# A Fourier mix followed by eight routed experts: one weaving step moved, one small copy moved to another engine, and shorter planning instructions

## The chip, the cores and the metric

The kernel runs on one core of one Trainium2 chip. The metric is device microseconds of one execution, lower is better; the time before is the median of 3 runs, 1263.31 us (1263.24 to 1265.31). The engines are named as the profile names them: PE is TensorE's matmul, PEld its weight load, DVE is VectorE, ACT is ScalarE, POOL is GpSimd, SP is SyncE, which here only issues DMAs, in order.

## The reference

`x` has 8 batches of 2496 rows of 256 numbers. Each batch goes through a Fourier transform along its rows and one along its columns, of which the real part is kept. The 19968 rows that come out are routed:

```python
logits = x @ w_gate                       # 8 experts
expert_idx = np.argmax(logits, axis=1)
gate_w = softmax(logits)[chosen expert]
h = np.maximum(x_of_expert @ w1[e], 0.0)  # 256 -> 1024
y = h @ w2[e]                             # 1024 -> 256
out = gate_w[:, None] * y
```

Everything is computed in float32.

## The kernel before, in words

**Stages of a batch.** `first(b)` (line 325) does the transform along the rows: three pieces `q`, each a load `xq` from `x` (line 289), adds and subtracts on DVE that fold it (lines 294 to 309), two halves of matmuls into a tile `s` (lines 311 to 321), an ACT copy of each half to `t` (line 321) and a store of `t` to a scratch tensor `Td` in DRAM (line 342), after which the next batch's piece is loaded (line 344). `first` is a generator with 12 steps. After them `ahead_of(b)` (line 929) issues two loads from `Td` in another layout, tile `t4` (`regroup`, line 351), the profile's `t<-Td`.

`second(b)` (line 361) is a generator with 19 steps. Its first matmul is `pr` on `t4` (line 371). Then come matmuls into `p2` (copied by ACT to `zz`, line 379) and ten blocks of 128 positions with matmuls into `p3`. From each `p3` the kernel takes: `zs`, copied by ACT (line 405); the 2 x 8 logits `lg`, copied by DVE (line 408); and two result rows per position, made by DVE with two instructions that read `p3` and `zs` into `rows` (line 410). ACT then fills the other half of these rows by mirroring (`mirror`, line 383; it is called for the block before, after `zs` of this one). After five blocks `route` (line 416) takes the maximum of the logits on DVE, makes a one-hot tile `oh`, ranks rows with small matmuls into `rk`, and computes the place of each row. `send` (line 462) then has POOL scatter 128 rows at a time into `Xs`, a DRAM tensor sorted by expert (line 236). 

`s`, `p2`, `p3`, `pr` and `rk` share one pool of three PSUM buffers, each a bank, so a matmul into one of them waits until the reads of the tile that had it before are done.

**Plans.** `plan` (line 478) works on one partition of DVE: it finds out how many blocks of a given size each expert can fill, and writes a table of up to MOST = 21 entries with the place and the expert of each block. SP reads the table to fetch rows (`xb`, line 535) and weights (`w_sb`, lines 545 and 547) of a block. Plans ask for 2 and 4 blocks in batch 0, 4 in batch 1, 3 in batch 2, 5 in each of batches 3 to 6, and 5, 7 and 21 in batch 7.

**Experts.** `experts` (line 729) goes through 66 blocks of 512, 256 or 128 rows. For each: transpose on DVE (line 583), a sign on ACT (line 586), matmuls into `ph` (or, for some 512-row blocks, seven products instead of eight, lines 614 to 658), relu on ACT or DVE (`hT`, lines 837 and 839), matmuls into `py`, a scaled ACT copy to `y` (line 891), a POOL scatter to the output. Row and weight fetches run up to three blocks ahead.

**What sets the order.** All instructions are written out in an order fixed in advance, and each engine runs its own in that order. `mixed(b)` (line 935) weaves `second(b)` with `first(b + 1)`:

```python
one, two = ahead_of(b + 1), second(b)
for _ in range(3):
    next(one, None); yield
for k, _ in enumerate(two):
    if k % 2:
        next(one, None)
    yield
yield from woven(close(b), one)      # close: the plans of batch b
yield from through(b)
```

The main loop (lines 996 to 1026) draws steps of `mixed(b)` in between the matmul groups of the experts of batch b - 1, about one step for each four to eight matmuls. Batch 0 is woven with batch 1 by a loop of its own (lines 990 to 993).

Of the kernel before, what the change touches and what calls it, by code (L numbers as in the profile page):

```python
# [15 lines left out]
ALU = mybir.AluOpType  # L16
ACTF = mybir.ActivationFunctionType
AX_X = mybir.AxisListType.X
# [17 lines left out]
E, F = 8, 1024  # L36
# [6 lines left out]
NY = H + 1  # L43
# [3 lines left out]
def free(ap, offset, *dims):  # L47
    return bass.AP(ap.tensor, ap.offset + offset, [list(ap.ap[0])] + [list(d) for d in dims])


def bc(ap, axis, n):
    shape = list(ap.shape)
    shape.insert(axis, n)
    return ap[tuple([slice(None)] * axis + [None])].to_broadcast(shape)
# [75 lines left out]
def rounds():  # L130

    want = [((256, 2), (128, 4)), ((256, 4),)] + [((512, B),)] * (B - 2)
    plan, used = [], 0

    def full(done, size):
        return max(0, -(-(done - used - E * (size - 1)) // size))

    for b in range(B):  # L140
        done = (b + 1) * S
        now = []
        for size, most in want[b]:
            k = min(full(done, size), most)
            if k:
                now.append((size, k, False))
            used += size * k
        if b == B - 1:
            k = full(done, BLK)
            used += BLK * k  # L150
            now.append((BLK, k, False))
            now.append((REST, (NT - used + E * (REST - 1)) // REST, True))
        plan.append(now)
    return plan
# [33 lines left out]
MOST = max(k for now in rounds() for _, k, _ in now)  # L188
# [27 lines left out]
def kernel(ctx: ExitStack, tc, x, w_gate, w1, w2, out):  # L216
    nc = tc.nc
    vec, act, pool = nc.vector, nc.scalar, nc.gpsimd

    def mm(o, lhsT, rhs, start=True, stop=True, **kw):  # L220
        nc.tensor.matmul(o, lhsT=lhsT, rhs=rhs, start=start, stop=stop, **kw)  # L221
# [47 lines left out]
    con, k = {}, 0  # L269
# [91 lines left out]
    def second(b):  # L361

        t4 = None

        def turn_last(h):

            nonlocal t4
            t4 = ahead.pop((b, "t4", h))
            n = min(HALF, NG - h * HALF)
            pr = pm_.tile([GP, HALF], F32, tag="m", name="pr")  # L370
            mm(pr[:, 0:n], con["rot"][:], t4[0:GP, 0:n, H])
            act.copy(t4[0:GP, 0:n, H], pr[:, 0:n])

        def group(g):
            i, n = g % HALF, LAST if g == NG - 1 else GP
            p2 = pm_.tile([128, 2, n], F32, tag="m", name="p2")
            for c in range(2):
                mm(p2[:, c], t4[0:GP, i, c * H:(c + 1) * H], con["m2"][:, c, 0:n])
            act.copy(zz[:, :, g * GP:g * GP + n], p2[:])
            if g == HALF - 1:  # L380
                turn_last(1)

        def mirror(rows, k):
            act.copy(free(rows[:], (k + 1) * W + D - 1, [-W, 2], [-1, H - 1]),
                     free(rows[:], k * W + 1, [W, 2], [1, H - 1]))

        turn_last(0)
        yield
        group(0)
        yield  # L390
        group(1)
        yield
        for h in range(2):
            rows = sp.tile([128, NSL, W], F32, tag="rows", name="rows")
            lg = sp.tile([128, NSL, E], F32, tag="lg", name="lg")
            for i in range(HW):
                w, k = HW * h + i, 2 * i
                if w + 2 < NG:
                    group(w + 2)
                p3 = pm_.tile([128, 2 * NY + 2 * E + 1], F32, tag="m", name="p3")  # L400
                z = zz[:, :, 128 * w:128 * (w + 1)]
                mm(p3[:, 0:NY + 2 * E], z[:, 0], con["rd"][:, 0, 0:NY + 2 * E], True, False, skip_group_check=True)
                mm(p3[:, NY:], z[:, 1], con["rd"][:, 1], False, True, skip_group_check=True)
                zs = sp.tile([128, NY + 1], F32, tag="zs", name="zs")
                act.copy(zs[:], p3[:, NY + 2 * E:])  # L405
                if i:
                    mirror(rows, k - 2)
                vec.tensor_copy(lg[:, k:k + 2], p3[:, NY:NY + 2 * E].rearrange("p (m e) -> p m e", m=2))  # L408
                for m, op in enumerate((ALU.add, ALU.subtract)):
                    vec.scalar_tensor_tensor(rows[:, k + m, 0:NY], p3[:, 0:NY], zs[:, 0:1], zs[:, 1:],  # L410
                                             op0=ALU.add, op1=op)
                yield
            mirror(rows, k)
            yield from route(b, h, rows, lg)
# [60 lines left out]
    bk = {n: bt[:, lo:hi] for n, (lo, hi) in where.items()}  # L475
    gone = bk["cap"]

    def plan(b, size, k, last):

        nonlocal gone  # L480

        def one(name, *dims, dt=F32):
            return cp.tile([1, *dims], dt, tag="p_" + name, name="p_" + name, bufs=2 if name == "gone" else 1)

        nb, ni = one("nb", E), one("ni", E, dt=I32)
        ce, ex, rb, n = one("ce", E), one("ex", E), one("rb", E), one("n", E)
        lo = one("lo", E, E)
        vec.tensor_tensor(nb[:], base[0:1], gone[:], op=ALU.subtract)
        vec.tensor_scalar(ni[:], nb[:], size - 1.0 if last else 0.0, None, op0=ALU.add)
        vec.tensor_scalar(ni[:], ni[:], size.bit_length() - 1, None, op0=ALU.logical_shift_right)  # L490
        vec.tensor_copy(nb[:], ni[:])
        vec.tensor_tensor(lo[:], bk["low"].rearrange("p (a b) -> p a b", a=E), bc(nb[:], 1, E), op=ALU.mult)
        vec.reduce_sum(ce[:], lo[:], axis=AX_X)
        vec.tensor_tensor(ex[:], ce[:], nb[:], op=ALU.subtract)
        yield
        vec.scalar_tensor_tensor(rb[:], ex[:], -float(size), gone[:], op0=ALU.mult, op1=ALU.add)
        ge, ei = one("ge", MOST, E), one("ei", MOST)
        val, eq, rw = one("val", MOST, E + 1), one("eq", MOST, E + 1), one("rw", MOST)
        vec.tensor_tensor(ge[:], bc(bk["i"], 2, E), bc(ce[:], 1, MOST), op=ALU.is_ge)
        vec.reduce_sum(ei[:], ge[:], axis=AX_X)  # L500
        yield
        vec.tensor_tensor(eq[:], bc(ei[:], 2, E + 1), bc(bk["e9"], 1, MOST), op=ALU.is_equal)
        vec.memset(val[:, :, E:E + 1], float(E * CAP))
        vec.scalar_tensor_tensor(val[:, :, 0:E], bc(bk["i"], 2, E), float(size), bc(rb[:], 1, MOST),
                                 op0=ALU.mult, op1=ALU.add)
        yield
        vec.tensor_tensor(val[:], val[:], eq[:], op=ALU.mult)
        vec.reduce_sum(rw[:], val[:], axis=AX_X)
        tab = cp.tile([1, 2, MOST], I32, tag="p_tab", name="p_tab", bufs=4)
        vec.tensor_copy(tab[:, 0], rw[:])  # L510
        vec.tensor_scalar(tab[:, 1], ei[:], E - 1.0, None, op0=ALU.min)
        if last:
            cnt = cp.tile([1, 1], I32, name="cnt")
            vec.tensor_copy(cnt[:], ce[:, E - 1:E])
            tabs["cnt"] = cnt
        if not last:

            vec.tensor_scalar(n[:], ex[:], -1.0, float(k), op0=ALU.mult, op1=ALU.add)
            vec.scalar_tensor_tensor(n[:], n[:], 0.0, nb[:], op0=ALU.max, op1=ALU.min)
            nxt = one("gone", E)  # L520
            vec.scalar_tensor_tensor(nxt[:], n[:], float(size), gone[:], op0=ALU.mult, op1=ALU.add)
            gone = nxt
        yield
        tabs[b, size, last] = tab
# [384 lines left out]
    def woven(*parts):  # L909
        parts = list(parts)  # L910
        while parts:
            for p in list(parts):
                if next(p, p) is p:
                    parts.remove(p)
                else:
                    yield

    def close(b):

        for size, k, last in rounds()[b]:  # L920
            yield from plan(b, size, k, last)

    def through(b):

        while waiting and waiting[0][0] == b:
            yield
        whole.add(b)

    def ahead_of(b):

        yield from first(b)
        regroup(b, 0)
        regroup(b, 1)

    def mixed(b):

        one, two = (ahead_of(b + 1) if b + 1 < B else iter(())), second(b)
        for _ in range(3):
            next(one, None)
            yield  # L940
        for k, _ in enumerate(two):
            if k % 2:
                next(one, None)
            yield
        yield from woven(close(b), one)
        yield from through(b)
# [133 lines left out]
```

## Time and profile before

| what | value |
|---|---|
| median of 3 runs | 1263.31 us (1263.24 to 1265.31) |
| the profiled execution's own time | 1264.13 us |
| its span, first to last instruction | 1262.3 us |
| PE busy | 1214.1 us (96%), 7289 matmul instructions |
| DVE busy | 777.0 us (62%) |
| ACT busy | 424.8 us (34%) |
| POOL busy | 446.1 us (35%) |
| mean granted TensorE clock | 0.971 |
| DMA | 249.79 MB, mean 198 GB/s |
| DVE copies of logits, line 408 | x80, 13.8 us, mean 173 ns |

A row of the costliest groups names the line, the engine, the operation, what it writes and reads and how often, then busy time and the mean of one, then the idle time of the engine just before these instructions and what ended most of it. A line of the waits view reads "who waited <- for what: us in total, times, longest". A timeline line gives start, duration, engine, line, operation, and in brackets the idle time before it with its releaser. A busy PE is not PE at its peak, and its ends are modelled.

### The profile page before, as it was taken

How to read it: one execution, taken by the hardware profiler on the slowest of the kernel's cores; microseconds unless marked ns; L12 is line 12 of the kernel's file. 1: busy time of each engine (PE TensorE's matmuls, PEld its weight loads, DVE VectorE, ACT ScalarE, POOL GpSimd, SP SyncE). 2: the span in 40 equal slices, each digit the busy share in tenths (PEclk: the TensorE clock that was granted, in tenths of full speed). 3: DMA queues.
4: the chain of work that ended last, by engine and by line, in shares of the span. 5: the costliest groups of instructions: out<-in, count | busy, mean ns of one | idle time of the engine just before them, and what ended most of it. 6: DMA issues, size and time to landing. Idle time of an engine off the chain costs nothing.

```text
span 1262.3 us, 22196 instructions
## 1 busy us (share of the span) xinstructions
PE 1214.1 (96%) x7289; PEld 1080.3 (86%) x7289; DVE 777.0 (62%) x1884; ACT 424.8 (34%) x1087; POOL 446.1 (35%) x527
## 2 busy tenths in 40 slices
PE   5769999999999999999999999999999999999997
PEld 3658988777788899888988898889999999999996
DVE  4546334443466788576866578686888784444663
ACT  1423332332243433433344333432333232222222
POOL 0245436154116512472225603472364241111112
PEclk6759999999999999999999999999999999999998
DMA  8869898765348454573336435453346338788887
GB/s 236 272 195 327 304 307 306 204 224 169 126 147 258 138 142 160 154 263 115 101 123 207 141 94 160 140 179 101 105 138 190 109 105 282 284 289 275 285 284 278
DMA packets 163216, 249.79 MB, mean 198 GB/s; under 512 B 118601, under 2 KB 130227, under 8 KB 143516
## 3 DMA queue, kind: packets, MB, share of 16 engines
q1 hardware_dynamic: 146327, 203.28, 51.0%
q0 software_dynamic: 15888, 42.14, 9.3%
q10 hardware_dynamic: 885, 2.94, 0.7%
q8 instruction: 59, 0.97, 0.3%
q14 instruction: 57, 0.47, 0.1%
HBM read 194.91 MB, written 54.83 MB: 198 GB/s over the span
## 4 chain that ended last, share of the span: by engine, by line
PE 62%; issue 17%; DVE 10%; DMA 5%; POOL 4%; ACT 2%; POOLq 0%; SPq 0%; DVEq 0%; ACTq 0%
PE py L221 18%; PE a L221 9%; PE c L221 7%; PE ph L221 6%; PE p L221 6%; PE b L221 5%; PE d L221 4%; PE s L221 3%; PE e L221 3%; POOL out_dram L236 3%; DMA t<-Td 1%; DMA xq<-in_x_dram 1%; POOL Xs L236 1%; DVE xT L583 1%; DMA Td<-t 1%
## 5 line engine op out<-in xcount | busy, mean ns | idle before, releaser
L236 POOL DMA_INDIRECT out_dram<-y,ro x163 | 160.9, 987 | 629.5 <-ACT y L679 299.6
L221 PE MATMUL py<-w_sb,hT 128*128 128x256 f32 x1504 | 340.3, 380 | 0.0
L221 PEld LDWEIGHTS py<-w_sb,hT 128*128 128x128 f32 x1504 | 281.2, 190 | 36.9 <-issue 1.0
L236 POOL DMA_INDIRECT Xs<-rows,pi x160 | 164.2, 1026 | 111.7 <-DVE rows L410 53.0
L221 PE MATMUL ph<-xT,w_sb 128*128 128x128 f32 (+2 forms) x992 | 173.1, 330 | 10.0 <-DVE ro L792 8.8
L221 PEld LDWEIGHTS ph<-xT,w_sb 128*128 128x128 f32 x992 | 137.6, 194 | 34.4 <-issue 16.5
L221 PE MATMUL a<-xT,w_sb 128*128 128x256 f32 (+1 forms) x512 | 117.9, 357 | 0.0
L837 DVE TENSOR_SCALAR hT<-ph 128x512 f32<-128x512 f32 x43 | 29.7, 691 | 127.9 <-PE ph L221 68.2
L586 ACT ACTIVATE xT<-xT 128x256 f32<-128x256 f32 (+1 forms) x94 | 36.5, 388 | 181.7 <-DVE xT L583 137.3
L221 PEld LDWEIGHTS a<-xT,w_sb 128*128 128x128 f32 x512 | 88.5, 190 | 10.0 <-DVE xT L583 0.3
L891 ACT ACTIVATE y<-py,xb 128x256 f32<-128x256 f32 x94 | 44.5, 473 | 153.8 <-PE py L221 152.1
L635 DVE TENSOR_TENSOR hT<-hT,b 128x512 f32<-128x512 f32 x57 | 39.2, 687 | 79.0 <-PE b L221 53.4
L408 DVE COPY lg<-p 128x16 f32<-128x16 f32 x80 | 13.8, 173 | 111.4 <-ACT zs L405 111.3
L645 ACT ACTIVATE hT<-a 128x512 f32<-128x512 f32 x57 | 34.0, 597 | 134.1 <-PE a L221 131.1
L221 PE MATMUL s<-xq,w 104*112 104x256 f32 (+2 forms) x208 | 62.4, 425 | 11.8 <-DVE xq L297 9.5
L469 POOL CAST pi<-due 128x1 int32<-128x1 f32 x140 | 42.2, 302 | 68.4 <-ACT due L468 68.4
L221 PE MATMUL a<-w_sb,hT 128*128 128x128 f32 x528 | 66.0, 276 | 0.0
L221 PEld LDWEIGHTS p<-table,t 120*128 120x128 f32 x352 | 54.7, 206 | 10.6 <-issue 3.1
L221 PEld LDWEIGHTS a<-w_sb,hT 128*128 128x128 f32 x528 | 63.1, 192 | 0.7
L221 PE MATMUL c<-xT,ws 128*128 128x256 f32 (+1 forms) x256 | 60.2, 362 | 1.2 <-DVE hT L641 0.4
L221 PE MATMUL p<-table,zz 128*128 128x145 f32 (+1 forms) x320 | 57.6, 306 | 3.6 <-DVE rows L410 2.4
L583 DVE STREAM_TRANSPOSE xT<-xb 128x512 f32<-128x512 f32 (+1 forms) x91 | 56.3, 631 | 7.0 <-DMA xb<-Xs 7.0
(149 smaller groups left out, 2103.2 us busy)
## 6 DMA issues: line engine op xcount, KB each, us to landing
w_sb<-in_moe_w_dram SPq DMA_DIRECT2D x132, 1024.0 KB, 6.9
xq<-in_x_dram SPq DMA_DIRECT2D x24, 896.0 KB, 8.9
xb<-Xs SPq DMA_DIRECT2D x112, 128.0 KB, 3.3
Td<-t SPq DMA_DIRECT2D x18, 448.0 KB, 3.3
t<-Td SPq DMA_DIRECT2D x8, 768.0 KB, 7.0
t<-Td SPq DMA_DIRECT2D x8, 640.0 KB, 9.3
xb<-Xs SPq DMA_DIRECT2D x52, 64.0 KB, 4.7
xb<-Xs SPq DMA_DIRECT2D x88, 32.0 KB, 4.8
```

The costliest lines, as they stand in the source:

```text
L221: nc.tensor.matmul(o, lhsT=lhsT, rhs=rhs, start=start, stop=stop, **kw)
L236: return unordered(pool.indirect_dma_start(out=dst, out_offset=bass.IndirectOffsetOnAxis(ap=idx, axis=0), in_=rows, in_offset=None, bounds ...
L408: vec.tensor_copy(lg[:, k:k + 2], p3[:, NY:NY + 2 * E].rearrange("p (m e) -> p m e", m=2))
L469: pool.tensor_copy(idx, due[:])
L583: vec.transpose(free(xT[:], 256 * h, [32, n // 32], [BIG, 2], [1, 32]), free(xb, 512 * h, [64, n // 32], [1, 2], [2, 32]))
L586: act.activation(odd, odd, ACTF.Copy, scale=-1.0)
L635: vec.tensor_tensor(h12, h11, b[:], op=add)
L645: act.activation(h11, a[:], ACTF.Relu)
L837: vec.tensor_scalar(o, ph[:], 0.0, None, op0=ALU.max)
L891: act.activation(y[:, i % 2], py[:], ACTF.Copy, scale=meta[:, i, 1:2])
```

## The change

Three edits. The logits leave PSUM by an ACT copy instead of a DVE copy, at the same place in the program, so behind `zs` and behind the mirror of the block before on ACT's queue. The plans work on as many entries as they ask blocks for (`k`) instead of MOST = 21. And `mixed` draws a step of the next batch's `first` at the even steps of `second`, beginning with its first, instead of at the odd ones.

```diff
                 act.copy(zs[:], p3[:, NY + 2 * E:])
                 if i:
                     mirror(rows, k - 2)
-                vec.tensor_copy(lg[:, k:k + 2], p3[:, NY:NY + 2 * E].rearrange("p (m e) -> p m e", m=2))
+                act.copy(lg[:, k:k + 2], p3[:, NY:NY + 2 * E].rearrange("p (m e) -> p m e", m=2))
                 for m, op in enumerate((ALU.add, ALU.subtract)):
                     vec.scalar_tensor_tensor(rows[:, k + m, 0:NY], p3[:, 0:NY], zs[:, 0:1], zs[:, 1:],
                                              op0=ALU.add, op1=op)
...
-        ge, ei = one("ge", MOST, E), one("ei", MOST)
-        val, eq, rw = one("val", MOST, E + 1), one("eq", MOST, E + 1), one("rw", MOST)
-        vec.tensor_tensor(ge[:], bc(bk["i"], 2, E), bc(ce[:], 1, MOST), op=ALU.is_ge)
-        vec.reduce_sum(ei[:], ge[:], axis=AX_X)
-        yield
-        vec.tensor_tensor(eq[:], bc(ei[:], 2, E + 1), bc(bk["e9"], 1, MOST), op=ALU.is_equal)
+        ge, val, eq = (one(name, MOST, E + 1)[:, 0:k] for name in ("ge", "val", "eq"))
+        ei, rw = (one(name, MOST)[:, 0:k] for name in ("ei", "rw"))
+        count = bk["i"][:, 0:k]
+        vec.tensor_tensor(ge[:, :, 0:E], bc(count, 2, E), bc(ce[:], 1, k), op=ALU.is_ge)
+        vec.reduce_sum(ei, ge[:, :, 0:E], axis=AX_X)
+        yield
+        vec.tensor_tensor(eq, bc(ei, 2, E + 1), bc(bk["e9"], 1, k), op=ALU.is_equal)
         vec.memset(val[:, :, E:E + 1], float(E * CAP))
-        vec.scalar_tensor_tensor(val[:, :, 0:E], bc(bk["i"], 2, E), float(size), bc(rb[:], 1, MOST),
+        vec.scalar_tensor_tensor(val[:, :, 0:E], bc(count, 2, E), float(size), bc(rb[:], 1, k),
                                  op0=ALU.mult, op1=ALU.add)
         yield
-        vec.tensor_tensor(val[:], val[:], eq[:], op=ALU.mult)
-        vec.reduce_sum(rw[:], val[:], axis=AX_X)
+        vec.tensor_tensor(val, val, eq, op=ALU.mult)
+        vec.reduce_sum(rw, val, axis=AX_X)
         tab = cp.tile([1, 2, MOST], I32, tag="p_tab", name="p_tab", bufs=4)
-        vec.tensor_copy(tab[:, 0], rw[:])
-        vec.tensor_scalar(tab[:, 1], ei[:], E - 1.0, None, op0=ALU.min)
+        vec.tensor_copy(tab[:, 0, 0:k], rw)
+        vec.tensor_scalar(tab[:, 1, 0:k], ei, E - 1.0, None, op0=ALU.min)
...
         for k, _ in enumerate(two):
-            if k % 2:
+            if k % 2 == 0:
                 next(one, None)
             yield
```

## The prediction

> **What bounds the kernel.** I read the page's slices first, then PE's waits, then the timeline at the longest waits.
>
> ```profile
> PE   5769999999999999999999999999999999999997
> ...
> PEclk6759999999999999999999999999999999999998
> ```
>
> Each digit is 1/40 of the span, 31.6 us. From the fifth slice on PE is full at the full clock. The windows of 40 us say the same: PE is idle 33.5 us before 120 us and some 7 us from there to the last window. So steps moved inside full stretches move nothing; what counts are the few gaps, and what an edit could open. PE's waits name the gaps:
>
> ```profile
> PE s L221 <- DVE xq L297: 9.5, 2, 6.5
> PE ph L221 <- DVE ro L792: 8.8, 1, 8.8
> PE pr L221 <- DMA t<-Td: 6.0, 3, 2.4
> PE rk L221 <- DVE oh L431: 4.1, 3, 2.6
> ...
> PE ph L221 <- DVE hT L837: 1.2, 1, 1.2
> ```
>
> The first row lies in the first 30 us, which the change leaves alone. Up to 87.37 us, the end of the 8.8 us wait, PE's other waits cost nothing: it then waits for the first expert rows, and these for POOL, which scatters batch 0 without a break from 53.47 to 81.11 us. Behind 87.37 us two gaps matter: at 121 us, and the last `pr` wait at 211.6 us.
>
> **The gap at 211.6 us (batch 3).** First PE, then SP's issues before it:
>
> ```profile
> 211.60 0.37 PE L221 MATMUL pr<-t,table 120*120 120x6 f32 x2 [2.32 <-DMA t<-Td]
> 211.83 1.13 PE L221 MATMUL p<-table,t 120*128 120x120 f32 x4
> 212.76 3.37 PE L221 MATMUL ph<-xT,w_sb 128*128 128x256 f32 x8
> 215.97 0.60 PE L221 MATMUL p<-table,t 120*128 120x120 f32 x4
> ```
> ```profile
> 190.53 0.31 SPq L342 DMA_DIRECT2D Td<-t  x1
> 190.94 0.38 SPq L289 DMA_DIRECT2D xq<-in_x_dram  x1
> 193.37 2.70 SPq L535 DMA_DIRECT2D xb<-Xs  x4
> 196.26 0.40 SPq L539 DMA_DIRECT2D xb<-Xs  x1
> 197.46 0.35 SPq L545 DMA_DIRECT2D w_sb<-in_moe_w_dram  x1
> 198.00 0.34 SPq L547 DMA_DIRECT2D w_sb<-in_moe_w_dram  x1
> 199.72 0.38 SPq L354 DMA_DIRECT2D t<-Td  x1
> ```
>
> PE waits 2.32 us, and the work behind runs at half speed: `p` x4 takes 1.13 where it later takes 0.60, `ph` x8 3.37 where it takes 1.89. By the chain's pieces (0.37, 0.99, 3.17 against 0.11, 0.44, 1.73) that is 2.2 us more, 4.5 in all. The Trainium skill ("TensorE: Matmul & The Clock Gate", Part 1) speaks against the second half: the clock falls after an idle window of about 3.4 us, and 2.32 is less. By that rule alone the gap would be worth 2.3 us and the whole sum would come to about -2.4. The row shows the slow matmuls, so I count them.
>
> What the move does here: `first` has 12 steps, three are drawn ahead, so its last falls on k = 16 instead of 17, and the two loads `t<-Td` on k = 18, ahead of the plans, instead of behind the first plan step. In the changed order of PE the last `s` half stands before a group of `py` (3.46 us in the chain) instead of behind it. The store to `Td` thus goes out near 187.1. It lands 3.3 us later (median of line 342; at most 8.3). The loads no longer stand behind rows and weights on SP, and go out between 190.7 and 195.7. They took 11.8 us here, so `t` is there by 203 to 207.5; PE asks at 209.3. **-4.5 us**; if only the idle part goes, -2.3.
>
> Each queue passed: on SP five row and two weight DMAs now stand behind the wait for `Td`. The rows go out near 193 to 198 instead of 193.4; their tile is transposed at 216.8, so there are over 15 us of cover. In batches 5 to 7 too the loads `t<-Td` (389.57, 535.03, 675.41) pass one fetch of rows and weights, delayed by one landing, 3 to 8 us. Cover: fetches run up to three blocks ahead, a 512 block takes some 25 us of PE, and between 200 and 850 us nothing waits for `w_sb` or `xb`. Without it, some 4 us for each of the three. DVE's folds and ACT's `t` copies of a step move with it, beside full PE. POOL's order is unchanged.
>
> **The gap at 121 us: shorter plans.** `ph` waits 1.15 us for an eviction on DVE that stands behind the plan of batch 1. Six instructions on 1x168 or 1x189 take 0.29 to 0.34 us, those on 1x64 0.21, on 1x8 0.15. With four entries they have 32 to 36 elements, about 0.18 each: 6 x 0.14 = 0.85, which leaves 0.3 of the wait, as nothing else stands before that eviction. **-0.85 us**, between -1.15 and 0. Other plans lie in time PE does not wait for, or in POOL's shadow before 87 us: nothing.
>
> **The logits copy.** It frees 80 x 173 ns on DVE, which is no bound, and costs ACT 80 copies of about 0.18 us (between the 0.17 of 120x6, line 372, and the 0.27 of 128x130, line 405): 14 us on an engine 34% busy. What it moves is a wait. Before, in a timeline of batch 0:
>
> ```profile
> 48.07 0.27 ACT L405 COPY zs<-p 128x130 f32<-128x130 f32 x1 [0.31 <-PE p L221]
> 48.24 0.41 ACT L384 COPY rows<-rows 128x254 f32<-128x254 f32 x1
> 48.37 0.17 DVE L408 COPY lg<-p 128x16 f32<-128x16 f32 x1 [1.27 <-ACT zs L405]
> 48.47 0.60 DVE L410 SCALAR_TENSOR_TENSOR rows<-p,zs 128x129 f32<-128x129 f32 x2
> ```
>
> The DVE copy does not use `zs`, yet waits for it: the program lets ACT and DVE read one `p3` bank only in turn. Now `rows` must wait for ACT's copy, which stands behind the mirror (line 384). An instruction behind a mirror starts 0.31 us after it (103.39 to 103.70), so the copy runs 48.55 to 48.73 and `rows` starts at 48.78, 0.3 later. Who waits for `rows`: the next mirror, the maximum of `route`, and PE when it wants the bank. From a `p3`'s last matmul to its freed bank I get 0.2 + 0.15 + 0.31 + 0.18 + 0.05 + 0.61 + 0.05 = 1.55 us, against 1.24 before.
>
> I counted, by bank and by PE's order, the matmul time between a `p3` and the next user of its bank, at full clock. Behind 87 us the old order has six places at 1.27 to 1.36 us; the new one has three, then six at 1.76 to 2.14, and some twenty at 2.5 to 3.0. Losses are 0.7 us in the new, about 0.6 in the old: **0**, bounds -0.6 and +1.5. In batch 0, where steps follow closely, each step's 0.3 partly adds up; I take 0.5 us at the end of the first `route`, from which POOL runs unbroken, so it reaches 87.37. Also one fold of batch 2 (94.06 to 95.40 in the chain, 1.34 us on DVE) now stands before the first transpose. POOL's scatters took 1.26, 1.57, 1.77 and 1.50 us instead of 0.97 where such folds ran beside: +0.3. In return that fold is gone from DVE before `rk` at 97.5, where PE waits 0.2. **+0.6 net**, from -0.7 (fewer slow scatters) to +2.3 (all five steps add up).
>
> **Sum**, against the profiled execution: 1264.13 - 4.5 - 0.85 + 0.6 = 1259.4. That execution is 0.8 above the median of the three runs, 1263.31, so I predict **1258.6** for the median.
>
> **Rivals.**
> - *The start or the clock eats it*: the gap goes but the start loses its 2.3, or the matmuls stay slow: 1263.3 - 4.5 - 0.85 + 2.3 = 1260.3, or 1263.3 - 2.3 - 0.85 + 0.6 = 1260.8; both together 1262.5. For: POOL's chain has no slack. Against: DVE has less to do there.
> - *The loads are no earlier*: before, they waited 1.4 us on SP though all issues were done, so the landing of `Td` counted too. If it stays late because DMA is busy (0.92 of its time from 200 to 220 us), only the plans are left: 1263.3 - 0.85 + 0.6 = 1263.1. Against: the store is 3.5 us earlier, and DMA was nearly idle just before 190.
> - *Slower: banks handed on through ACT's queue.* Place: all ten `p3` of seven batches among expert work. If the copy also stands behind a relu (0.60) or a `t` copy (0.58), a bank takes 2.7 us instead of 1.55: three places lose 1.4 each, the six at 1.76 to 2.14 lose 3.7 together, those from 2.5 about 1.2: 9 us, 8.3 more than counted, so 1266.9; at 3.0 us 1273. It decides from about 2.6 us on. For: ACT is strictly in order. Against: ACT is idle two thirds of the time and mostly waits for PE.
>
> **How the numbers follow.** A measurement of this kernel can tell about 0.2%, 2.5 us, so faster means below 1260.8. Chances: the forecast and a little around it (1256.0 to 1260.7) 0.60; start, clock or late loads 0.25; slower by the banks 0.13, the rest 0.02 for steps between. The range takes the lower bounds in part (-4.5 - 1.15 - 0.7 - 0.6, to 1256.4, a little below) and goes up to 1265, which leaves out most of the slower case. Faster 0.60, same 0.26, slower 0.14.
>
> **What would show it.** Right: no `pr <- DMA t<-Td` wait after 100 us, full clock from 200 to 220 us, the `hT` wait at 121 us at 0.3, the first `ph` near 88 us. Wrong: `PE p` or `PE s <- DVE rows` (or a bank wait without a name) of several us behind 100 us; a first `ph` later than 89.5 us; or rows or weights waited for between 200 and 700 us.

## The result, and the profile after

| | before | after |
|---|---|---|
| median | 1263.31 us (1261.85 to 1265.39, 9 runs) | 1259.27 us (1255.38 to 1261.30, 9 runs) |
| the profiled execution | 1264.13 us, span 1262.3 | 1258.56 us, span 1256.8 |
| mean granted clock | 0.971 | 0.976 |

The ratio is **0.9964, 95% interval 0.995 to 0.9978**: 4 us faster, where 1258.6 us was forecast. All line numbers behind 496 are one higher in the changed kernel (a row fetch `xb` is line 536, the relu on DVE 838).

The experiments ran in three batches, on chips that the record numbers 8, 2 and 13, where the unchanged kernel takes 1281.44, 1278.75 and 1280.83 us instead of 1263. I call them the experiment chips; the number of the chip of the table above, here the first chip, is not on record. Chip 8 had the weave alone, the loads first, the copy ahead of the mirror, and weave with short plans; chip 2 the unchanged kernels, the copy alone and the short plans alone; chip 13 the moved tiles and the three kernels with `ge` kept. Each ratio is against the unchanged kernel of its own batch, but traces of different batches come from different chips, and the unchanged kernel has a trace from chip 2 alone. Ratios are of fast runs: one execution in 29 of the unchanged kernel on chip 13 took 2481 us and is left out of them.

**On chip 2 the same change makes the kernel slower: 1.0069 (1.0045 to 1.0093).** Most of what follows is about this difference.

The slices of the page of the changed kernel, first:

```profile
PE   5759999999999999999999999999999999999997
...
PEclk6869999999999999999999999999999999999998
```

PE is full from the fifth slice on, as before; in the granted clock the third slice has gone from 5 to 6, the second from 7 to 8. PE's waits (who <- for what: us in total, times, longest):

```profile
PE s L221 <- DVE xq L297: 12.1, 3, 6.3
PE ph L221 <- DVE xT L584: 11.1, 1, 11.1
...
PE pr L221 <- DMA t<-Td: 1.4, 2, 1.2
```

Of the `pr` waits, 6.0 us before, 1.4 is left, all in the first 100 us. The `ph` wait for `hT` is not in the list any more. The first two rows, the waits of the start, have grown, by 2.6 and 2.3 us. PE's timeline where the gap of batch 3 was, and SP's issues ahead of it:

```profile
209.62 0.28 PE L221 MATMUL pr<-t,table 120*120 120x6 f32 x2
...
210.85 1.90 PE L221 MATMUL ph<-xT,w_sb 128*128 128x256 f32 x8
```
```profile
187.60 0.31 SPq L342 DMA_DIRECT2D Td<-t  x1
...
190.94 2.33 SPq L354 DMA_DIRECT2D t<-Td  x2
194.47 3.67 SPq L536 DMA_DIRECT2D xb<-Xs  x4
...
199.93 0.36 SPq L546 DMA_DIRECT2D w_sb<-in_moe_w_dram  x1
```

`pr` has no wait, and the eight `ph` behind it take 1.90 us instead of 3.37. On SP the two loads stand right behind the store; rows and weights come after them.

**Where the 5.5 us between the two spans lie**, from the starts of the same evictions in both traces: the changed kernel is 2.1 us late at the first relu (91.2 us), 0.5 late at 192 us, 3.5 early at 701 us, 4.0 at 847, 4.3 to 4.5 at 1252, 5.5 at the last `y`. Between 192 and 701 us one half of `s` stands before or behind a group of matmuls, so that single readings there differ by 0.9.

### The profile page after: what moved, and what is told of

Read it like the earlier page. It is cut to its first block, busy times and chain, and to the rows that moved or that the text cites. A ratio compares the mean times of both kernels' runs of the same rounds, so it can differ in the third digit from the quotient of the medians.

```text
span 1256.8 us, 22295 instructions
## 1 busy us (share of the span) xinstructions
PE 1208.1 (96%) x7289; PEld 1076.3 (86%) x7289; DVE 759.6 (60%) x1804; ACT 431.3 (34%) x1167; POOL 447.5 (36%) x527
## 4 chain that ended last, share of the span: by engine, by line
PE 82%; DVE 9%; DMA 4%; ACT 2%; issue 2%; POOL 0%; SPq 0%; POOLq 0%; DVEq 0%; ACTq 0%
PE py L221 25%; PE ph L221 13%; PE a L221 11%; PE c L221 9%; PE p L221 6%; PE b L221 6%; PE d L221 5%; PE e L221 4%; PE s L221 3%; DMA xq<-in_x_dram 1%; DVE xT L584 1%; DMA Td<-t 1%; DVE y L684 1%; DMA Xs<-rows,pi 1%; DVE hT L639 1%
## 5 line engine op out<-in xcount | busy, mean ns | idle before, releaser
L410 DVE SCALAR_TENSOR_TENSOR rows<-p,zs 128x129 f32<-128x129 f32 x160 | 48.9, 348 | 128.8 <-ACT lg L408 124.8
L469 POOL CAST pi<-due 128x1 int32<-128x1 f32 x140 | 45.1, 322 | 65.5 <-ACT due L468 65.5
L221 PEld LDWEIGHTS s<-xq,w 104*112 104x112 f32 x208 | 38.5, 204 | 26.3 <-DVE xq L297 10.8
```

The lines of the kernel that those rows point to most:

```text
L469: pool.tensor_copy(idx, due[:])
```

## The experiments

### Where the experiment chips differ

The kernels on record as "before" and "after" ran again, unchanged.

> The kernel before, unchanged, for a trace from the chip on which the experiments run: there it takes about 1281 us instead of 1263, and the theories need to know where. If the 18 us are a property of that chip, they stand at the same places as in the experiments: some 8 us between 116 and 130 us, and 1 to 2 us each near 410, 560, 705, 847 us, where 2 MB of weights arrive.

> The changed kernel, unchanged, on the chip of the experiments. The two experiments that held the weave and the short plans ran 0.6 to 0.8% above before there, the weave alone 0.3% below. Theory A (the logits copy and the plans cost little, as on the first chip): ratio to before 0.995 to 0.998. Theory B (on this chip the short plans cost some 10 us, whatever the logits copy does): ratio 1.004 to 1.009, with the added waits on DVE near 415, 560 and 705 us as in the kernel with the logits on DVE.

The profiled execution of the unchanged kernel, on chip 2, took 1274.75 us, near the low end of the 24 others there (median 1278.75, 1274.43 to 1285.79). Against the first chip's trace it is 3.7 us late at 121 us, 4.9 at 410, 6.4 at 701 and 8.5 at 840: the expected places, and smaller amounts. In the experiments' traces ACT or DVE often starts 2 to 7 us after the record of the product that it reads has ended, and PE then waits for it; POOL's scatters run on meanwhile. In the unchanged kernel DVE reads `ph` at 128.65 us, 4.6 us after the record of its last matmul; in the two traces of the first chip no such delay behind 80 us is over 2.0. The trace of the unchanged kernel on chip 2 also holds only 905 of the 1001 updates of PE's semaphore (the signal of one engine to another that its work is done) that the first chip's trace holds, so releasers there are less certain; a missing record does not show a late signal. Why engines start late, the runs do not show.

The changed kernel took 1287.74 us there (10 runs): theory B of its expectation.

### The weave alone, and the loads first with the store left late

```diff
-            if k % 2:
+            if k % 2 == 0:
```

> The kernel before with the weaving edit alone (a step of the next batch's first at the even steps of second). Theory: this edit alone takes away the batch 3 wait for t near 211 us with the slow matmuls behind it, worth 3 to 4.5 us, and hardly moves the start: first ph 87.4 to 88.2 us (87.37 before), time 1259 to 1260.5. Rival (the start is late because of this edit, since a fold of batch 2 now runs on DVE ahead of the first transpose and beside POOL's scatters): first ph near 89 to 89.6 as in the changed kernel, time 1260.5 to 1262. The DVE wait for hT near 121 us should stay (1.15 us before), since the plans are the old ones.

1277.24 us against 1281.44, ratio 0.9967 (0.9949 to 0.9985): 4.2 us, the size forecast for the gap. The wait at the gap is gone:

```profile
219.77 0.28 PE L221 MATMUL pr<-t,table 120*120 120x6 f32 x2
```

In the unchanged kernel of chip 2 it is there:

```profile
215.18 0.37 PE L221 MATMUL pr<-t,table 120*120 120x6 f32 x2 [1.90 <-DMA t<-Td]
```

The first `ph` starts at 88.48 us, 87.20 in the unchanged kernel of chip 2: between theory and rival. `ph` still waits 1.9 us for `hT` behind the plan of batch 1, as expected.

```diff
             yield
+        next(one, None)
         yield from woven(close(b), one)
```

> The kernel before, weaving at odd steps as before, but the last step of the next batch's first, which issues the two loads from Td, is drawn right behind the loop, so these loads stand on SP ahead of the row and weight fetches of batch 3 while the store to Td is no earlier than before (190.5 us). Theory A (the place of the loads is what counts; the store lands about 3.3 us after its issue): loads go out near 194 to 196, t is there by 208, the wait at 211 us is gone, time 1259 to 1260.5. Theory B (the landing of the store is what counts, the loads waited 1.4 us for it on SP at 199.7): loads go out near 199 to 200 as before, the wait near 211 stays at 2 us or more, rows and weights of the next block are late too, time 1262.5 to 1265.

1276.56 us, ratio 0.9965 (0.995 to 0.9981), the same gain. SP's issues in it:

```profile
198.01 0.31 SPq L342 DMA_DIRECT2D Td<-t  x1
...
201.37 1.80 SPq L354 DMA_DIRECT2D t<-Td  x2
204.31 4.59 SPq L535 DMA_DIRECT2D xb<-Xs  x4
```

The store goes out 3.5 us later than in the unchanged kernel of chip 2 (194.47; the kernel is late as a whole there), 18.7 us before PE asks for `t`, and yet `pr` does not wait:

```profile
216.66 0.28 PE L221 MATMUL pr<-t,table 120*120 120x6 f32 x2
```

In the unchanged kernel it is 18.8 us from the store to where PE asks, and `pr` waits 1.90. So theory A holds: an earlier store is not needed, the loads only have to stand ahead of the row and weight fetches on SP.

### The logits copy

Alone, in the kernel before:

```diff
-                vec.tensor_copy(lg[:, k:k + 2], ...)
+                act.copy(lg[:, k:k + 2], ...)
```

> The kernel before with the logits copy on ACT alone. Theory (rows wait for the copy behind the mirror, the first route and POOL's scatters end later): first ph 88.5 to 89.5 us where before has 87.4, time 1 to 2 us above before, ratio 1.0008 to 1.0016. Rival (DVE is relieved and nothing waits): first ph as before or earlier, ratio at or below 1.000.

1281.56 us against 1278.75, ratio 1.0019 (1.0002 to 1.0036): a cost of 2.4 us by the ratio, just above the prediction's upper bound of 2.3 at the start, with an interval from 0.3 to 4.6. The first `ph` is at 93.12 us, later than expected. How much of that is the copy's is not shown: from the last put of POOL's scatter to the first `ph` there are 12.3 us, and the four kernels with the copy on DVE and long plans differ among themselves there, from 7.5 to 10.4. Then the changed kernel with the copy ahead of the mirror:

> The changed kernel with ACT's logits copy put directly behind zs, ahead of the mirror. Theory (rows wait for the copy because it stands behind the mirror of 0.41 us): rows can start about 0.4 us earlier per step, the first route ends earlier by up to 1.5 us, first ph 88 to 88.6 us, time 1257.8 to 1258.6. Rival (the place of the copy is of no matter, the fold delays the start): first ph near 89.5, time as the changed kernel, 1259.3.

1288.76 us, ratio 1.0058 (1.0041 to 1.0075), which its interval does not tell apart from the changed kernel's, and the first `ph` at 92.54 us: neither the time nor the start that was expected. But the mechanism shows in two timelines of batch 0, the changed kernel on the first chip and this one:

```profile
49.49 0.27 ACT L405 COPY zs<-p 128x130 f32<-128x130 f32 x1 [0.60 <-PE p L221]
49.65 0.41 ACT L384 COPY rows<-rows 128x254 f32<-128x254 f32 x1
49.96 0.17 ACT L408 COPY lg<-p 128x16 f32<-128x16 f32 x1
50.17 0.61 DVE L410 SCALAR_TENSOR_TENSOR rows<-p,zs 128x129 f32<-128x129 f32 x2 [1.65 <-ACT lg L408]
```
```profile
47.80 0.27 ACT L405 COPY zs<-p 128x130 f32<-128x130 f32 x1 [0.30 <-PE p L221]
47.96 0.18 ACT L406 COPY lg<-p 128x16 f32<-128x16 f32 x1
48.03 0.42 ACT L384 COPY rows<-rows 128x254 f32<-128x254 f32 x1
48.17 0.61 DVE L410 SCALAR_TENSOR_TENSOR rows<-p,zs 128x129 f32<-128x129 f32 x2 [1.35 <-ACT lg L406]
```

From `zs` to `rows` it is 0.68 us with the copy behind the mirror, 0.37 with it in front, and 0.40 before. From the fifth `zs` to the maximum of `route` it is 1.20 or 1.21 us in every kernel with the copy behind the mirror, on whichever chip, and 0.90 or 0.91 in all others. **The 0.3 us per step is the mirror's**, and an exchange of two lines takes it away; that this gains time is not shown.

With weave and short plans but the copy left on DVE:

> The changed kernel with the logits copied by DVE again, so the weave and the short plans alone. Theory (the logits copy behind the mirror on ACT is what delays the start): first ph 87.4 to 88.2 us instead of 89.55, time 1.3 to 2 us below the changed kernel, 1257.3 to 1258. Rival 1 (the start is late because of the woven fold): first ph near 89.5, time as the changed kernel, 1259.3. Rival 2 (the freed DVE helped behind 87 us): over 1260.

1290.07 us, ratio 1.008 (1.005 to 1.011), and the first `ph` at 91.85 us. By the expectation it should have been 5 to 6 us below before; it is 8.6 above. That is over 1260 on the scale of the expectation, which rival 2 had for a DVE no longer freed; but the changed kernel itself, with DVE freed, is as slow on chip 2, so that is not the cause. What is common to both are the weave, which gains alone, and the plans.

### The short plans

> The kernel before with the short plans alone. Theory A: 0.5 to 1.4 us faster than before (the wait for hT near 121 us and the one near 841 us go), ratio 0.9988 to 0.9997. Theory B (short plans cost on this chip): 8 to 13 us slower than before, ratio 1.006 to 1.01, with PE waits for DVE's hT near 415, 560 and 705 us of 2 to 3 us each.

1288.06 us, ratio **1.0066 (1.0041 to 1.0092)**: the smallest edit, forecast at -0.85 us, costs 9.3 us by the medians on chip 2. All four kernels that held the short plans had been slow, and the three without them had not. But the edit does one thing that no part of my prediction looked at: it makes one scratch tile larger.

```diff
-        ge, ei = one("ge", MOST, E), one("ei", MOST)
+        ge, val, eq = (one(name, MOST, E + 1)[:, 0:k] for name in ("ge", "val", "eq"))
```

The tiles laid out behind it, weights, `xq`, `t` and others, move by 96 bytes. So the two were parted: the move without the instructions, and the instructions without the move (`ge` kept at 21 x 8).

> The kernel before with one scratch tile of the plans (ge, 21 x 8 numbers on one partition) made 21 x 9, of which 21 x 8 are used as before. No instruction changes, but all tiles that are laid out behind it (xq, t, rows, weights, xb, xT, hT, y) move by 96 bytes, to just the places they have in the changed kernel. On the chip of the experiments the four kernels with the new plans lost 0.6 to 0.8% and the three without them did not. Theory S (the moved tiles cost there): ratio 1.005 to 1.009. Theory I (the plan instructions cost): ratio 0.999 to 1.001.

> The kernel before with the short plans alone, but with the scratch tile ge kept at 21 x 8, so that every tile outside the plans stays where it was. Theory S (moved tiles cost): 0.5 to 1.5 us faster than before, ratio 0.9985 to 0.9998. Theory I (the plan instructions cost): ratio 1.005 to 1.009 as with the moved tiles.

The moved tiles alone: 1280.92 us against 1280.83, ratio 0.9999 (0.9984 to 1.0013), nothing. The short instructions without the move: 1286.24 us, ratio **1.0036 (1.0021 to 1.0052)**. Both ran on chip 13. Theory S fails, the plans' instructions cost; whether they cost more with the tiles moved is not settled, since the two intervals overlap and 1.0066 is from chip 2. The whole change and the change less the copy, both without the move:

> The changed kernel, all three edits, with ge kept at 21 x 8, so with every tile outside the plans where it was before. Theory S: the loss of the changed kernel on this chip (ratio 1.0069) goes, ratio 0.997 to 0.9995 (weave alone 0.9967, logits copy alone 1.0019, plans a little). Theory I: ratio 1.004 to 1.009.

> The last one with the logits copied by DVE again: weave and short plans, tiles where they were before. Theory S: the fastest of all, ratio 0.9945 to 0.9965, 2 to 3 us below the kernel with the copy on ACT. Theory I: ratio 1.003 to 1.008, as with moved tiles (1.008).

1287.06 us, 1.0046 (1.0028 to 1.0065), and 1286.16 us, 1.0048 (1.0033 to 1.0063): both slow, as theory I has it, and neither told from the plans alone. The copy back on DVE did not gain the 2 to 3 us that I expected beside short plans.

**Where the plans' time lies.** The kernel with the moved tiles alone (chip 13) and the one with the short plans (chip 2) have every tile outside the plans at the same place, and differ in the shape of DVE's instructions in the plans only. By the starts of the same evictions, at the times of the moved tiles, the short plans are 5.1 us later at the first relu, 3.0 at 420 us, 8.1 at 576, 11.5 from 718 to 847, 8.5 at 861, 8.2 at the end. So part of the loss is there before the first relu, and of that 4.2 us are there at the fifth `zs`, ahead of any plan: scatter of the start. Against the kernel with `ge` kept, also on chip 13, it is 2.0 us at the first relu and 8.4 at the end. From POOL's last put to the first `ph` all seven kernels with short plans there take 11.5 to 14.4 us, the five with long plans 7.5 to 12.3: a second place of the loss, of which the runs do not show the cause. PE's waits from 100 to 1240 us, with the short plans and with the moved tiles alone:

```profile
PE c L221 <- DVE hT L642: 9.5, 6, 2.8
```
```profile
PE c L221 <- DVE hT L641: 4.1, 3, 2.6
```

And one of these waits in the timeline of the short plans, with the ACT instruction that should have started just behind 420.7 us, where the product `a` ended:

```profile
424.34 1.13 PE L221 MATMUL c<-xT,ws 128*128 128x256 f32 x4 [2.79 <-DVE hT L642]
```
```profile
422.92 0.60 ACT L646 ACTIVATE hT<-a 128x512 f32<-128x512 f32 x1 [4.83 <-PE e L221]
```

These waits, 2.0 to 2.8 us, come at 424, 572 and 722 us, each while SP fetches the rows of a batch's first 512 block. The other kernels with short plans on the experiment chips have two or three of them, of 0.6 to 2.9 us. In the five with long plans, PE's wait for `c` at these places is at most 0.2 us, and a wait of `a` for ACT in its stead at most 1.7; they have one of 2.6 to 2.8 us for `c` near 850 us, which is at most 1.5 with the short plans. Behind the first relu, then, the loss is a late start of ACT or DVE at fixed places in the program, longer with one shape of the plans than with the other, on all three chips. What ties its length to the plans stays open: the plans' instructions take less time here too, and the fetch stands at the same place on SP.

## Why the prediction was right or wrong, point by point

- **The gap at 211 us, -4.5: right in size, its reason half right.** The 2.32 us of waiting and the slow matmuls went; the count from 192 to 701 us is -4.0, the edit alone on chip 8 -4.2. I gave the earlier store and the earlier place of the loads as one step. The place alone does it.
- **Its second half, 2.2 us at half clock, was rightly counted, but it is not always there.** Kernels without the move waited at this `pr` between 0.85 and 2.36 us on the experiment chips. The copy alone, and the moved tiles alone:

```profile
222.86 0.37 PE L221 MATMUL pr<-t,table 120*120 120x6 f32 x2 [0.85 <-DMA t<-Td]
...
223.81 1.90 PE L221 MATMUL ph<-xT,w_sb 128*128 128x256 f32 x8
```
```profile
219.00 0.37 PE L221 MATMUL pr<-t,table 120*120 120x6 f32 x2 [1.86 <-DMA t<-Td]
...
219.95 3.38 PE L221 MATMUL ph<-xT,w_sb 128*128 128x256 f32 x8
```

  Behind 0.85 us `ph` runs at full speed, behind 1.86 at half. So by these traces I estimate the same edit at 1 to 4.5 us. It was also luck that the slow half was there: the last section shows that it hangs on where the wait falls, not on its length alone. A small slip besides: without the slow half the recorded sum comes to -2.3 - 0.85 + 0.6 = -2.55, not about -2.4. Why the weave gained nothing beside the short plans is open. A short wait is not the reason: the kernel with short plans and `ge` kept still waited 2.36 us at this `pr`, with `ph` at 3.21 us behind it, and had 1.0036 without the weave and 1.0048 with it, both on chip 13.
- **The plans, -0.85: about right on the first chip, wrong in sign on the others.** On the first chip, in the trace with all three edits, the 1.15 us wait at 121 us is gone altogether (0.3 was to stay), and one of 0.24 us at 841 us with it; the plans alone were not run there. On the experiment chips the term is +5.4 us without the moved tiles (chip 13) and +9.3 with them (chip 2), by the medians. The step that failed: I took a shorter instruction for one that can only cost less, and kept no bound above zero.
- **The logits copy: right in mechanism, its size at the start too small.** The 0.3 us per step is in the trace to a hundredth. The first `ph` came 2.18 us later where 0.6 was forecast, at the edge of the bound of 2.3, and past the 89.5 us that I had named as a sign of error. By pieces, before and after on the first chip: first `zs` +0.85 (nothing that the change touches stands ahead of it; PE's wait for `xq`, the loading of `x`, is 2.6 us longer, and in the experiments' traces the first `zs` comes anywhere from 39.1 to 41.5 us), first to fifth `zs` +0.57, to the maximum +0.29, POOL's first to last put +0.50, the rest 0. Of these the 0.29 is the copy's beyond doubt; the 0.57 may be its steps adding up (I put 0.5 for both together), but in the experiment chips' kernels with the copy on DVE the same stretch took 6.2 to 6.8 us in most and up to 12 in one, so it may also be scatter. The slow puts took 0.5 where I put 0.3, and the load stage's 0.85 I had not counted.
- **Behind 87 us the copy costs nothing: nearly so on the first chip.** No PE wait for DVE's `rows`, and none without a name, lies behind 92 us. But `p` and `s` wait five times for the bank that ACT's copy of `s` (line 321) has to free, 1.6 us in all, where the kernel before has no such wait. The weave alone has 0.6 of it, so some is the weave's; the rest may be the copy's, within the bound of +1.5. The rival of banks handed on through ACT, at 8.3 us, did not come true.
- **The rival "the loads are no earlier"** failed too: 3.3 us after the store both loads went out.
- **What I did not see**: the end. The last 1.3 us of the 5.5 come from the last blocks, behind 1252 us, where the kernel branches; I have no cause for them from one trace. The last fall to half clock is at 1253.38 us before and 1250.08 after, some 1 us later in the program, which may be part of it.

The forecast thus held for the chip it was made on: the gap and the plans by terms that were about right, the sum in part by luck, since a start 1.5 us worse than forecast was made up by an end 1.3 us better, for which I have no cause. Of the rival in which the start or the clock eats the gain, the start did lose nearly its 2.3 us; the clock did not. The forecast does not hold for the experiment chips, and nothing in the one profile that I had could have told so.

## What to carry to other kernels

A load that PE will ask for soon belongs ahead of bulk fetches on an in-order queue; try its place alone before moving the work that feeds it. Work out what a copy stands behind on its new engine: here an exchange of two lines saves the 0.3 us of each step. And measure a gain of 0.4% with each edit apart, and on more than one chip: of the three edits only the weave, 0.9967 alone, gained where each was timed alone, and the change as a whole was 0.4% faster in one place and 0.7% slower in the other.

## What the runs showed of the hardware that was not expected

- **Whether a wait brings the half clock depends on where it falls, not on its length alone.** At the `pr` of batch 3, waits of 0.85 and 1.35 us left the eight `ph` behind them at 1.90 us; waits of 1.86, 1.90, 2.32 and 2.36 us brought them to 3.38, 3.02, 3.37 and 3.21. Yet there is no edge between 1.35 and 1.86 us. In the unchanged kernel on chip 2 a wait of 1.88 us left eight `ph` at full speed, and the 2.79 us at 424.34 us shown above left the matmuls behind it at 1.03 to 1.13 us:

```profile
122.04 1.99 PE L221 MATMUL ph<-xT,w_sb 128*128 128x256 f32 x8 [1.88 <-DVE hT L837]
```

  The clock records show a grid instead. From 84 to 1240 us every stretch at half clock lasts 3.41 or 6.83 us, and within one trace the starts lie whole multiples of 3.413 us apart: in the changed kernel on chip 2 they are at 90.45, 128.00, 151.89, 424.96 and 721.92 us, that is 11, 18, 98 and 185 such windows behind the first. Where the grid lies differs from trace to trace. The window ahead of the slow `ph` of batch 3 on the first chip, and the slow one (PE busy is the second number, the granted clock the third from the end):

```profile
208.91:212.32 3.41, 1.09 (x7) 0.60 (x5) 0.58 (x1) 0.77 (x2) 2.77 (x4) 1.00 1.09 410
212.32:215.73 3.41, 3.41 (x9) 2.81 (x10) 0.00 (x0) 0.36 (x1) 2.63 (x5) 0.50 1.01 420
```

  I laid this grid over the 13 traces that have such a stretch, and took the windows at full clock from 87 to 1200 us. All 34 in which PE was busy for less than 45% were followed by half clock, 7 of the 12 between 45 and 52%, and none above. So a wait of 2 us costs the slow matmuls when it lies in one window, and not when it is split over two. (PE's ends are modelled, so the shares are estimates.) The Trainium skill ("TensorE: Matmul & The Clock Gate", Part 1) has a free-running window of about 3.4 us, which agrees, and says that the clock falls after at least one idle window; here a window in which PE was busy for 1.09 of 3.41 us was enough, and the measurement decides.
- **ACT or DVE can start 2 to 7 us after the record of the product that it reads has ended**, on the three experiment chips and not on the first (at most 2.0 us in its two traces). In the unchanged kernel, 4.6 us at 128.65 us. The runs do not show why.
- **A shift of most tiles by 96 bytes** moved nothing: 0.9999 (0.9984 to 1.0013), on chip 13.
